# Reordering bias reads and three conversion steps at the start of an attention stage

## The chip, the cores and the metric

The kernel runs on one core of one Trainium2 chip. The metric is the device time of one execution in microseconds. Three runs of the kernel before gave 890.56, 889.25 and 890.60 us, with a median of 890.56 us. The engines are TensorE (PE, its weight load is PEld), VectorE (DVE), ScalarE (ACT), GpSimd (POOL) and SyncE (SP), whose queue issues nearly all DMA transfers here.

## What the kernel computes

Three stages follow one another. The first is attention with a learned relative-position bias over 4 batches, 8 heads, 576 positions and 64 dimensions a head:

```
scores = scale * q @ k.T                                # [4, 8, 576, 576]
x      = log1p(|i - j|) / log1p(max(i, 1))              # [576, 576]
bias   = relu(x * w1 + b1) @ w2                         # [576, 576, 8]
attn   = softmax(scores + bias) @ v
```

Then come a gated block, `((x @ w1) * (x @ w2)) @ w3 @ w_out` on 2304 rows, and a second block of an input projection, a softmax-weighted unit, a normalisation and an output projection. Weights arrive as 64-bit words and are turned into 32-bit numbers on the chip in five steps each.

## The kernel before, in words

The bias is made first, in 36 steps (`Bias.run`, L168). One step makes 16 rows of the bias for all heads: VectorE and ScalarE make masks (L162, L160), TensorE sums them (L191), ScalarE or VectorE copies the sum to a tile `rs` (L198, L196), and SP writes that tile to one of three DRAM tensors, `bias_d` (`write`, L47 through `Chip.load`). The steps take the rows in the order `list(range(32, 36)) + list(range(32))`, so that rows 384 to 511, the row groups 24 to 31, are written by the last eight steps, 28 to 35. After each step `beside(n)` puts other work in the queues: the first query, key and value tiles, bias reads, and steps of the first weights' conversion (`EARLY`).

Attention then runs over 16 pairs (four head pairs by four batches) of ten rounds each. Round s belongs to pair n = s // 10, and k = s % 10 is its unit. Units 0 to 8 are one 128 by 576 tile of scores each; round 9 has none. In a round (`slot`) the program hands each engine, in this order, the work of tiles of different ages: ScalarE copies transposed tiles (L478) and takes the exponential of the tile of two rounds ago (L381); VectorE adds the bias to the tile of the round before (L374), makes inverse sums (L388, L389), and makes the low parts of the transposed tiles (L492); GpSimd scales tiles (L393); TensorE makes the scores (L363, or L79 to L81 for unit 0), the transposes of a tile of eight rounds ago (L403) and the products with the values (L446). Each engine works through its own queue in order.

SP issues in order too. Query and key tiles are split by GpSimd into a high and a low part (L54, L57) and copied by SP into the layout that TensorE needs (`prep`; L51): the query copies (four `q<-qh`, two `qz<-ql`) of pair n + 1 go out in the third round of pair n, its four key copies `k<-kr` in the fifth, behind the load of the query and key tile of the pair after (`qkr`, 640 KB). What goes out in a round is kept in a list, `later[s]`, which `slot(s)` empties in order. Pair 1's first score tile with copied keys is that of round 11.

`load_bias(p, k)` has SP read the bias rows of unit k from `bias_d`. Units 1 to 4 are the first head's rows, 5 to 8 the second's; unit 4 and unit 8 take rows 384 to 511, unit 3 and unit 7 rows 256 to 383. A read of unit 4 is one DMA of 288 KB, one of unit 7 or 8 two DMAs of 256 and 32 KB. A read has to wait until the writes of its rows have landed.

The five conversion steps of the first two weight tiles (`first_ab`) are ten instructions in a list, which `some(n)` hands out: two behind bias step 29, five behind step 33, and the last three behind round 4 (`FILL`): one of line 72 and two of line 73, each a VectorE operation on 128 by 512 words with two inputs in SBUF. Their results are read after the last score round, from round 161 on.

Of the kernel before, what the change touches and what calls it, by code (L numbers as in the profile page):

```python
# [202 lines left out]
class Attention:  # L203
# [6 lines left out]
    LAG = 8  # L210
    AVLAG = 2
    EARLY = {29: 2, 33: 5}
    FILL = 4
    AHEAD = {(2, 3): (1,), (2, 7): (3,), (3, 3): (0,), (3, 5): (5,), (3, 8): (7,)}

    def __init__(self, ch, i, bias, x_d, ga):
# [255 lines left out]
    def slot(self, s):  # L472
        NP = len(self.pairs)
        n, k = divmod(s, 10)
        SQ = self.SQ
        ev, self.EV = self.EV, []
        for hi, lo, src in ev:
            self.nc.scalar.copy(hi, src)  # L478
        while self.OUT:
            self.nc.scalar.copy(*self.OUT.pop())  # L480
        if s - 2 in SQ:
            self.exp(*SQ[s - 2])
        if s - 1 in SQ:
            self.add_bias(*SQ[s - 1])
        if s - 3 in SQ:
            self.inverse(*SQ[s - 3])
            if SQ[s - 3][1] % 2:
                self.normalise(*SQ[s - 4])
            if SQ[s - 3][1] % 2 or SQ[s - 3][1] == 8:
                self.normalise(*SQ[s - 3])  # L490
        for hi, lo, src in ev:
            self.nc.vector.tensor_tensor(out=lo, in0=src, in1=hi.bitcast(F), op=ALU.subtract)  # L492
        if n < NP and k < 9:
            self.scores(n, k)
        tn, tu = divmod(s - self.LAG, 10)
        if 0 <= tn < NP:
            for u in self.TU[tu]:
                self.transposes(tn, u)
        an, au = divmod(s - self.LAG - 1 - self.AVLAG, 10)
        if 0 <= an < NP:  # L500
            self.values(an, self.AV[au], s)
        if k == 4 and n + 2 < NP:
            self.load_qk(n + 2)
        for fn in self.later.pop(s, []):
            fn()
        if n < NP:
            if n + 1 < NP and k < 4:
                self.prep(n + 1, k, s + 1)
            if k in (5, 6):
                self.prep(n, k - 1, s + 1)  # L510
            if k == 7 and n + 1 < NP:
                self.load_v(n + 1)
            p, b = self.pairs[n]
            if p + 1 < NPH:
                for j in self.AHEAD.get((b, k), ()):
                    self.load_bias(p + 1, *((j, j + 1) if j else (0,)))
            if s == self.FILL:
                self.some(len(self.fill))


class Gated:
# [735 lines left out]
def tile_kernel(tc, i, out):  # L1257
    with tc.manual_schedule(), tc.tile_pool(name="dram", bufs=1, space=DRAM) as dp:
        x_d = [dp.tile([2, DM, S], F, name="x_d%d" % b) for b in range(NB)]
        x2_d = [dp.tile([DM, TC], F, name="x2_d%d" % c) for c in range(NC)]  # L1260
        gw_d = dp.tile([FF, DM], F, name="gw_d")
        g_d = [dp.tile([FF, TC], F, name="g_d%d" % c) for c in range(NC)]
        ch = Chip(tc)

        ga = Gated(ch, i, x_d, x2_d, gw_d, g_d)
        ga.open_keep()
        bias = Bias(ch, i, dp)
        bias.open()
        at = Attention(ch, i, bias, x_d, ga)
        at.open_left()  # L1270

        at.load_qk(0)
        for n in range(2):
            at.load_ab(n)
        at.load_v(0)

        def beside(n):

            at.start(n)
            if n == 7:  # L1280
                at.load_bias(0, 0)
            if n in (24, 27):
                at.load_bias(0, *{24: (1, 2), 27: (5, 6)}[n])
            if n in (32, 33):
                at.load_bias(0, {32: 3, 33: 7}[n])
            at.some(at.EARLY.get(n, 0))

        bias.run(beside)
        bias.ctx.close()
        at.open_right()  # L1290
        scored = 10 * len(at.pairs)
        for s in range(at.slots()):
            n = s - scored
            if n == 0:
                at.left.close()
                at.psl.close()
                ga.open_left()
            if n == ga.MID:
                at.top.close()
                ga.open_mid()  # L1300
            if s == 3:
                at.load_bias(0, 4)
                at.load_bias(0, 8)
            at.slot(s)
            ga.early(n)
        at.right.close()
        at.psr.close()
        ga.open_right()
        ga.run()
        ga.tail.close()  # L1310
        ga.psr.close()
        ga.psl.close()
        so = Solu(ch, i, ga, out)
        so.open()
        so.run()
        so.ctx.close()
        ga.right.close()
        ga.left.close()
# [64 lines left out]
```

## Time and profile before

| | |
|---|---|
| profiled execution | 891.37 us |
| its span | 889.6 us |
| median of three runs | 890.56 us |
| TensorE, VectorE, ScalarE, GpSimd busy | 96%, 72%, 57%, 35% of the span |
| mean granted TensorE clock | 0.994 of full speed |

The span runs from the first instruction to the last; 1.77 us of the profiled execution lie around it. A time such as 64.86 is counted from the start of the span. Bias steps fill the first 59 us, attention goes on to about 310 us. In a row of a timeline the start comes first, then how long it took; "[5.64 <-DVE st L374]" says that the engine had idled 5.64 us and what ended that. For a DMA, the row of SP is its issue; "us to landing" is from the start of the issue to the end of the transfer.

### The profile page before, as it was taken

To read this page: it belongs to the slowest core of one execution; us is meant where nothing else is said; L and a number is where in the kernel's file an instruction comes from. 1 tells how busy PE (TensorE), PEld (TensorE's weight loads), DVE (VectorE), ACT (ScalarE), POOL (GpSimd) and SP (SyncE) were. 2 spreads that over 40 slices of the span, in tenths; PEclk is the share of its full clock that TensorE was granted. 3 is DMA by queue.
4 is the path that set the end of the run, shared out by engine and by line. 5 is a ranking of instruction groups with operands and counts; after the bars stand their busy time and mean duration, and the time that the engine had idled before them with its cause. 6 is when DMAs were issued, how large, how long until landed. Compare 5 with 4: busy or idle time off the path is not lost.

```text
span 889.6 us, 15987 instructions
## 1 busy us (share of the span) xinstructions
PE 853.7 (96%) x5430; PEld 769.2 (86%) x5430; DVE 638.0 (72%) x1517; ACT 506.0 (57%) x1073; POOL 307.9 (35%) x379
## 2 busy tenths in 40 slices
PE   7978999999999889989999999999999999999998
PEld 3548999999999789888888999999998788888886
DVE  8998999999999788997652777353454855555552
ACT  6887999999899845443322445333344544444432
POOL 3038888889898700000000000000344333333300
PEclk9998999999999999999999999999999999999999
DMA  6997897897987656767413587443134011111001
GB/s 227 300 304 184 240 268 200 252 261 192 302 222 211 189 169 210 229 216 230 157 60 133 189 278 257 152 166 122 63 131 128 27 42 41 44 40 48 24 24 48
DMA packets 93538, 146.31 MB, mean 164 GB/s; under 512 B 11792, under 2 KB 58256, under 8 KB 93456
## 3 DMA queue, kind: packets, MB, share of 16 engines
q1 hardware_dynamic: 86064, 134.96, 49.7%
q10 hardware_dynamic: 7392, 10.33, 3.3%
q8 instruction: 43, 0.70, 0.3%
q14 instruction: 39, 0.32, 0.1%
HBM read 81.93 MB, written 41.30 MB: 139 GB/s over the span
## 4 chain that ended last, share of the span: by engine, by line
PE 78%; DVE 8%; ACT 2%; DMA 2%; issue 2%; SPq 0%; POOL 0%; ACTq 0%; DVEq 0%; POOLq 0%
PE op L446 9%; PE tp L403 8%; PE sp L363 7%; PE ab L79 7%; PE ab L81 7%; PE ab L80 7%; PE o L80 4%; PE o L79 4%; PE o L81 4%; PE x L80 3%; PE x L81 3%; PE x L79 3%; PE hx L79 2%; PE hx L80 2%; PE hx L81 2%
## 5 line engine op out<-in xcount | busy, mean ns | idle before, releaser
L79 PE MATMUL ab<-x,ab 128*128 128x384 f32 x320 | 109.0, 341 | 5.1 <-DVE a L791 5.1
L492 DVE TENSOR_TENSOR etl<-tp,eth 128x512 fp32r<-128x512 f32 (+1 forms) x160 | 99.4, 630 | 14.0 <-ACT eth L478 11.8
L81 PE MATMUL ab<-x,ab 128*128 128x384 f32 x320 | 108.0, 337 | 1.1 <-DVE ab L650 1.1
L80 PE MATMUL ab<-x,ab 128*128 128x384 f32 x320 | 107.9, 337 | 0.1
L393 POOL TENSOR_SCALAR e<-e,st 128x576 f32<-128x576 f32 x128 | 95.0, 752 | 27.6 <-DVE st L389 24.7
L381 ACT ACTIVATE e<-e,st 128x576 f32<-128x576 f32 x128 | 100.1, 782 | 6.1 <-DVE st L374 6.1
L478 ACT CAST eth<-tp 128x512 fp32r<-128x512 f32 (+1 forms) x160 | 85.2, 543 | 22.6 <-PE tp L403 16.1
L374 DVE CUSTOM_DVE_ANT_0 e<-sp,bt 128x576 f32<-128x576 f32 x128 | 95.5, 747 | 3.2 <-DMA bt<-bias_d 1.9
L403 PE MATMUL tp<-idt,e 128*128 128x128 f32 x576 | 87.3, 274 | 4.3 <-DVE ell L492 1.6
L940 POOL MEMSET onef<- 128x128 f32 x1 | 0.2, 204 | 232.0 <-DVE mean L925 232.0
L363 PE MATMUL sp<-k,q 128*128 128x288 f32 x256 | 73.5, 302 | 7.3 <-DVE st L374 6.1
L403 PEld LDWEIGHTS tp<-idt,e 128*128 128x128 f32 x576 | 69.5, 141 | 6.7 <-DVE ell L492 1.8
L363 PE MATMUL sp<-k,qz 128*128 128x288 f32 x256 | 72.4, 298 | 0.0
L791 DVE TENSOR_TENSOR a<-ab,a 128x384 f32<-128x384 f32 x48 | 26.6, 555 | 63.6 <-ACT a L790 63.3
L79 PEld LDWEIGHTS ab<-x,ab 128*128 128x128 f32 x320 | 60.4, 189 | 8.2 <-DVE a L791 8.2
L446 PE MATMUL op<-eth,v 128*128 128x288 f32 x256 | 65.6, 337 | 0.4 <-ACT o L480 0.4
L80 PE MATMUL x<-gl,wf 128*128 128x384 f32 x192 | 64.7, 337 | 0.5 <-DVE gl L62 0.5
L81 PE MATMUL x<-gh,wf 128*128 128x384 f32 x192 | 64.5, 336 | 0.0
L79 PE MATMUL x<-gh,wf 128*128 128x384 f32 x192 | 64.5, 336 | 0.0
L81 PEld LDWEIGHTS ab<-x,ab 128*128 128x128 f32 x320 | 60.3, 189 | 1.6 <-DVE ab L650 1.4
L80 PEld LDWEIGHTS ab<-x,ab 128*128 128x128 f32 x320 | 60.4, 189 | 0.4 <-DVE x L750 0.4
L1231 ACT ACTIVATE o<-o,st 128x512 f32<-128x512 f32 x18 | 12.4, 688 | 79.5 <-PE o L81 29.4
(213 smaller groups left out, 2341.4 us busy)
## 6 DMA issues: line engine op xcount, KB each, us to landing
bias_d<-rs SPq DMA_DIRECT2D x36, 295.5 KB, 4.1
qkr<-in_qk SPq DMA_DIRECT2D x16, 640.0 KB, 5.6
k<-kr SPq DMA_DIRECT2D x64, 144.0 KB, 5.6
g_d<-a ACTq DMA_DIRECT2D x48, 192.0 KB, 2.8
gl<-g_d SPq DMA_DIRECT2D x48, 192.0 KB, 2.6
x_d<-o SPq DMA_DIRECT2D x58, 144.0 KB, 4.0
q<-qh SPq DMA_DIRECT2D x64, 128.0 KB, 2.7
raw<-in_wo SPq DMA_DIRECT2D x16, 512.0 KB, 4.3
```

The lines of the kernel that those rows point to most:

```text
L79: mm(out, a[0], b[0], start=first, stop=False, skip_group_check=more)
L80: mm(out, a[0], b[1], start=False, stop=False, skip_group_check=more)
L81: mm(out, a[1], b[0], start=False, stop=last, skip_group_check=more)
L363: nc.tensor.matmul(ps[:, half, :HS], w[("q", "qz")[x]][:, h, q * 128 : q * 128 + 128], w["k"][:, h, half * HS : half * HS + HS], start=x = ...
L374: self.nc.vector.tensor_tensor_reduce(out=halves(e), in0=ps[:, :, :HS], in1=halves(self.BT[(self.pairs[n][0], k)]), scale=-0.125, scalar=3e38,
L381: self.nc.scalar.activation(e, e, AF.Exp, bias=st[:, c : c + 1], scale=-1.0, accum_out=st[:, 2 + 2 * c : 3 + 2 * c])
L393: self.nc.gpsimd.tensor_scalar(out=e, in0=e, scalar1=st[:, c : c + 1], scalar2=1.0, op0=ALU.mult, op1=ALU.mult)
L403: tr = lambda c, src: nc.tensor.transpose(ps[: src.shape[1], c * 128 : c * 128 + 128], src, self.idt)
L446: nc.tensor.matmul(w["op"][:, half, :HS], lhs, rhs, start=c == 0 and x == 0, stop=c == 4 and x == 1)
L478: self.nc.scalar.copy(hi, src)
L492: self.nc.vector.tensor_tensor(out=lo, in0=src, in1=hi.bitcast(F), op=ALU.subtract)
L791: nc.vector.tensor_tensor(out=a, in0=ps[:, 1, :TC], in1=a, op=ALU.mult)
```

## The change

The read of unit 4's bias rows for the first head pair is no longer issued behind all six query copies of round 2, but as the third of that round's list, behind two of them. The two DMAs of unit 7 leave bias step 33 and stand ahead of round 3, where unit 4's read was, before those of unit 8. The last three conversion steps leave round 4 for rounds 20, 30 and 40, one each.

```diff
-    FILL = 4
+    FILL = (20, 30, 40)
...
-            if s == self.FILL:
-                self.some(len(self.fill))
+            if s in self.FILL:
+                self.some(1)
...
-            if n in (32, 33):
-                at.load_bias(0, {32: 3, 33: 7}[n])
+            if n == 32:
+                at.load_bias(0, 3)
             at.some(at.EARLY.get(n, 0))
...
+            if s == 2:
+                at.later[s].insert(2, lambda: at.load_bias(0, 4))
             if s == 3:
-                at.load_bias(0, 4)
+                at.load_bias(0, 7)
                 at.load_bias(0, 8)
             at.slot(s)
```

## Rows read from the trace of the kernel before

**Rows 1.** Busy time by stretch: us, five engines, granted clock, DMA share, GB/s.

```profile
68.00:70.00 2.00, 0.80 (x3) 0.80 (x4) 1.59 (x6) 0.82 (x3) 0.00 (x0) 0.50 0.97 183
...
76.00:300.00 224.00, 222.94 (x1763) 218.85 (x1763) 208.28 (x608) 206.76 (x490) 196.80 (x223) 1.00 0.81 226
...
310.00:312.00 2.00, 1.18 (x8) 0.95 (x8) 2.00 (x4) 1.42 (x4) 1.22 (x2) 1.00 0.35 118
312.00:314.00 2.00, 1.51 (x7) 1.51 (x8) 2.00 (x5) 0.67 (x2) 0.00 (x0) 0.59 0.03 9
```

**Rows 2.** Chain of waits around the idle stretch: start, us, what.

```profile
64.86 3.38 DMA bt<-bias_d
...
69.20 3.51 PE sp L363 x12
...
75.96 0.77 PE sp L363 x4
```

**Rows 3.** Timelines of TensorE and VectorE, 69 to 106 us.

```profile
69.20 0.61 PE L363 MATMUL sp<-k,q 128*128 128x288 f32 x1 [5.64 <-DVE st L374]
...
71.52 0.76 DVE L374 CUSTOM_DVE_ANT_0 e<-sp,bt 128x576 f32<-128x576 f32 x1 [0.20 <-PE sp L363]
...
75.41 0.45 DVE L492 TENSOR_TENSOR ell<-sp,elh 64x64 fp32r<-64x64 f32 x2
...
106.01 0.29 PE L363 MATMUL sp<-k,q 128*128 128x288 f32 x1
```

**Rows 4.** SP's issues and the last `rs` on ScalarE, 58 to 68 us.

```profile
58.15 0.93 SPq L47 DMA_DIRECT2D bt<-bias_d  x2
...
58.44 0.76 ACT L198 ACTIVATE rs<-ps,cst 128x591 f32<-128x591 f32 x1
...
59.68 0.45 SPq L47 DMA_DIRECT2D bias_d<-rs  x1
...
62.95 1.23 SPq L51 DMA_DIRECT2D q<-qh  x2
...
67.44 0.59 SPq L51 DMA_DIRECT2D k<-kr  x1
```

**Rows 5.** KB, us to landing; issued 56.43, 57.78, 58.62, 59.68, 64.86, 67.44.

```profile
bias_d<-rs SPq DMA_DIRECT2D x1, 295.5 KB, 3.1
...
bias_d<-rs SPq DMA_DIRECT2D x1, 295.5 KB, 3.7
...
bt<-bias_d SPq DMA_DIRECT2D x1, 32.0 KB, 3.9
...
bias_d<-rs SPq DMA_DIRECT2D x1, 295.5 KB, 4.5
...
bt<-bias_d SPq DMA_DIRECT2D x1, 288.0 KB, 3.4
...
k<-kr SPq DMA_DIRECT2D x1, 144.0 KB, 7.8
```

**Rows 6.** The same, issued 77.82, and second key copies issued 99.06 and 129.81.

```profile
q<-qh SPq DMA_DIRECT2D x1, 128.0 KB, 2.2
...
k<-kr SPq DMA_DIRECT2D x1, 144.0 KB, 6.4
...
k<-kr SPq DMA_DIRECT2D x1, 144.0 KB, 5.0
```

**Rows 7.** VectorE's conversion steps and a GpSimd scaling beside them, timelines.

```profile
62.88 1.90 DVE L72 SCALAR_TENSOR_TENSOR rab<-rab 128x512 uint32<-128x512 uint32 x1
64.71 1.75 DVE L73 SCALAR_TENSOR_TENSOR rab<-rab 128x512 uint32<-128x512 uint32 x2
...
64.23 1.69 POOL L393 TENSOR_SCALAR eab<-eab,st 128x576 f32<-128x576 f32 x1
```

**Rows 8.** Such a scaling, 80 to 160 us (busy, mean ns, idle); line 72 elsewhere (ns).

```profile
L393 POOL TENSOR_SCALAR eab<-eab,st 128x576 f32<-128x576 f32 x6 | 4.5, 748 | 0.0
...
L72 DVE SCALAR_TENSOR_TENSOR cm<-raw,cm x46: 674/692/694, 313.6 to 556.5; 128x512 uint32<-128x512 uint32 x46
```

## The prediction

> **What bounds the kernel now.** I read the busy time by stretch first. From 76 to 300 us TensorE works 222.94 of 224 us [rows 1]: behind round 11 attention has no room, and what is lost or won before it arrives at the end nearly whole. So the question is when round 11 starts. The chain of waits shows the last gap ahead of it: the DMA of unit 4's bias rows, issued at 64.86, lands 3.38 us later [rows 2], and TensorE idles 5.64 us until 69.20 [rows 3]. During it the granted clock fell to 0.50 [rows 1], the lower of its levels (1.2 against 2.4 GHz), and twelve score products from 69.20 took 3.51 us [rows 2], where four take 0.77 from 75.96 on.
>
> Round 11's scores start at 75.96 [rows 2]. They need three things. VectorE must have emptied a score buffer: its two operations from 75.41 end at 75.86 [rows 3], and that came last. Second, the query copies. Third, the first two key copies: the second was issued at 67.44 [rows 4] and landed 7.8 us later [rows 5], at 75.2. The two ends that matter stand only 0.6 us apart. That decides this case: cutting the bias wait gains 0.6 us at most as long as the key copies land when they do.
>
> **Unit 7's two DMAs leave step 33.** Their issue takes SP 0.93 us at 58.15 [rows 4], just ahead of the last two bias writes. The last `rs` is ready at 58.44 + 0.76 = 59.20 [rows 4], so the last write goes out at about 59.23 where it went out at 59.68 [rows 4]. On the DMA engines, which are full there, the write issued at 57.78 landed at 61.5, unit 7's last read at 58.62 + 3.9 = 62.5, and the last write at 59.68 + 4.5 = 64.2 [rows 4, 5]. Without the 1.0 us of the reads that last write lands at about 63.2. Bounds: 59.23 + 3.1 = 62.3 by the quickest such write [rows 5], and 64.2 if nothing changes. I take 63.2, for the engines were full.
>
> **Unit 4's read moves past four query copies.** Two copies and their pitch are 1.23 us [rows 4], so four are 2.5 us, and the place itself comes at about 62.0. But unit 4's rows are those of the last eight bias steps, so the read has to wait for that last write, at the head of SP's queue, and whatever stands behind it there waits too. So it is issued at 63.2, not at 62: 1.65 us earlier than 64.86. It then takes between 2.2 us, which a query copy takes in a quiet stretch [rows 6], and its own 3.4 us [rows 5]. I take 3.1, nearer to its own row, since the last write's successors are still moving. It lands at 66.3 (65.4 to 67.6) instead of 68.24, and rounds 5 to 10 come 1.9 us sooner: round 11 could start at about 74.0.
>
> The Trainium skill (DMA: Bandwidth & Descriptors, "Anatomy of one DMA", measured for DMAs that GpSimd issues) counts a fixed 2.0 us plus the bytes at 436 GB/s. By it, as an estimate, 288 KB would take 2.7 us and land at 65.9; by the row it is 66.6. Neither end would move the start of round 11, by what follows.
>
> **What is late next: the key copies.** They stand in the same queue behind all of this. From unit 4's issue to that of the second key copy it was 67.44 - 64.86 = 2.58 us [rows 2, 4]. Now there are four query copies (2.5 us) and unit 7's two DMAs (1.0 us with the pitch) between them besides: 63.2 + 2.5 + 1.0 + 2.6 = 69.3 us, 1.85 us later than 67.44. Of its 7.8 us [rows 5] some was the backlog of full DMA engines (share 0.97 at 68 to 70 [rows 1]); the same copy of later pairs takes 6.4 or 5.0 [rows 6]. The wait of about 1.2 us in SP lets that backlog shrink, while the bytes ahead of the keys stay the same. I take 7.0: between the copy's own row and the 6.4. So it lands at 76.3; bounds 69.3 + 5.0 = 74.3 and 69.3 + 7.8 = 77.1. Round 11 starts at 76.35: **0.4 us later than before** (bounds -1.6 and +1.2), though the bias came 1.9 us sooner.
>
> **Unit 7's read, now late.** It goes out at 63.2 + 0.6 + 2.5 = 66.3 and with 3.4 lands at 69.7. VectorE took unit 7 at 71.52 [rows 3], 3.3 us behind the bias's landing; now that is 66.3 + 3.3 = 69.6. A wait of 0.1, bounds 0 and 1, lies inside the 2.3 us by which the keys are later than the rest, and costs nothing. If the keys were early, it would cost its length.
>
> **The three conversion steps.** In round 4 they ran from 62.88 to 66.46 [rows 7], under the wait for the bias, for nothing; under a bias that lands at 66.3 they would cost 0.1 to 0.2 us, which the keys hide too. Taking them away gains nothing. In rounds 20, 30 and 40 there is no wait to hide them, but in these rounds VectorE has no tile of a unit 9 to add bias to, and in 224 us it idles 15.7 [rows 1], about 1 us in each pair of 15.0 us (round 11 at 75.96, round 31 at 106.01 [rows 2, 3]). One step takes 0.69 undisturbed [rows 8] and up to 1.90 beside GpSimd [rows 7]. So each costs between 0 and about 0.9; I take 0.1, as 0.69 is under 1, and 0.3 for the three. A gain is excluded there: work is only added.
>
> **The sum.** 0.4 + 0.3 = +0.7 us. The profiled execution would go from 889.6 + 1.77 = 891.37 to 892.1. It lies 0.81 above the median of 890.56, so the median becomes **891.3 us**. A measurement of this kernel can tell about 0.2%, 1.8 us: no change that can be told.
>
> **The rivals.**
>
> A second drop of the clock (the other side). TensorE now idles twice, about 3.7 us for the bias and 2.3 us for the keys. The 5.64 us cost it the clock, and so did a stretch where it worked 1.18 of 2 us, after which the clock was 0.59 [rows 1]. If the wait for keys makes it fall, rounds 11 to 13 run at half. Twelve products at half took 3.51 us [rows 2], at full they are some 1.6 to 2.3 (0.77 for four, with the start of the first): a price of 1.2 to 1.9, 1.5 here. That gives 890.56 + 0.7 + 1.5 = 892.8, slower. It decides from a keys' wait of some 2 us on. Against it: 2.3 us is under half of 5.64.
>
> Conversion steps that meet GpSimd. Line 72 took 1.90 for 0.69, and the scaling beside it 1.69 for 0.75 [rows 7, 8]. If each of the three delays the products with the values by 0.9, the sum is 0.4 + 2.7: 893.7. Against it is VectorE's idle time. The Trainium skill (GPSIMD Engine Reference, "1. Specifications") says that GpSimd shares its SBUF interfaces with VectorE and contends with VectorE instructions of two SBUF inputs, as these three are. The trace agrees by the 1.69 us; by that rule the steps leave an empty stretch for one where GpSimd works 197 of 224 us [rows 1], and this rival is the time.
>
> Keys land early. If DMAs drain while SP waits, the second key copy lands in 5.0 us, at 74.3, and round 11 starts there: -1.6 + 0.3, 889.3. For it: later pairs. Against: every byte ahead of the keys is still there.
>
> The change doesn't do what it says. If the last write still lands at 64.2, unit 4's read goes out 0.6 us sooner only, and the keys 2.85 later, landing at up to 78.1: +1.5 to +2.1 with keys as slow as 7.0 to 7.8 us and no loss elsewhere, 892.3. Against it are the 1.0 us of DMA time that left.
>
> **How the numbers follow.** Forecast 0.42, with its own range 890.2 to 892.2; clock 0.25; GpSimd 0.08; keys early 0.17; no earlier read 0.08. Faster than 888.8 would take keys as early as the bound and no cost of the steps, or a gain that I don't see: 0.13. Slower than 892.3: most of the clock's case, GpSimd's, half of the last: 0.33. Between: 0.54. The range from 888.7 to 893.1 leaves about 0.1 out on each side.
>
> **What would show it.** Right: SP issues unit 4's read right behind two query copies, close to the landing of the last bias write at about 63.2; TensorE's first gap is about 3.7 us instead of 5.64; a new gap stands ahead of round 11's scores, ended by the key copies' landing near 76.3; VectorE has three lone operations of lines 72 and 73 near 91, 106 and 121 us, with no gap of TensorE behind them. Wrong: round 11's scores before 75, or a read of unit 4 that is issued before the last write has landed; then the gain is up to 1.9 us and more, and the time below 889.

## The result, and the profile after

The changed kernel is slower: a median of 894.22 us over 7 runs against 890.23 us over 7 runs of the kernel before, a ratio of 1.0054 (95% interval 1.0040 to 1.0069). Its profiled execution took 894.85 us, with a span of 893.1 us.

SP's issues in the changed kernel, start and us:

```profile
59.88 1.36 SPq L51 DMA_DIRECT2D q<-qh  x2
63.20 0.33 SPq L47 DMA_DIRECT2D bt<-bias_d  x1
...
66.04 2.05 SPq L47 DMA_DIRECT2D bt<-bias_d  x4
68.19 0.38 SPq L47 DMA_DIRECT2D qkr<-in_qk  x1
...
69.12 0.59 SPq L51 DMA_DIRECT2D k<-kr  x1
```

Its transfers issued at 58.81 (the last bias write), 63.20 (unit 4's read) and 69.12 (the second key copy), with KB and us to landing:

```profile
bias_d<-rs SPq DMA_DIRECT2D x1, 295.5 KB, 4.2
...
bt<-bias_d SPq DMA_DIRECT2D x1, 288.0 KB, 3.5
...
k<-kr SPq DMA_DIRECT2D x1, 144.0 KB, 8.6
```

Both query copies are out at 61.24. Then SP stands still for 1.96 us until the last bias write has landed, at 58.8 + 4.2 = 63.0, and issues unit 4's read at 63.20. That read lands at 66.7, against 68.24 before [rows 2]. The second key copy goes out 1.7 us later than before [rows 4] and lands at 69.12 + 8.6 = 77.7, against 75.2 before [rows 5].

The busy time by stretch, with the columns of [rows 1]:

```profile
62.00:64.00 2.00, 1.16 (x8) 0.79 (x6) 0.54 (x4) 1.28 (x4) 1.92 (x3) 1.00 0.28 76
...
68.00:70.00 2.00, 2.00 (x9) 1.75 (x8) 1.31 (x6) 1.44 (x5) 1.25 (x2) 0.50 0.93 252
...
72.00:74.00 2.00, 0.44 (x2) 0.14 (x1) 0.75 (x3) 1.97 (x7) 1.17 (x2) 1.00 1.01 230
74.00:76.00 2.00, 1.93 (x10) 1.87 (x10) 1.92 (x10) 0.90 (x3) 0.89 (x2) 0.64 0.98 198
76.00:78.00 2.00, 0.36 (x2) 0.00 (x0) 1.65 (x6) 0.58 (x1) 1.97 (x3) 0.50 0.58 151
78.00:80.00 2.00, 1.97 (x9) 1.98 (x10) 0.63 (x1) 0.00 (x0) 2.00 (x3) 0.50 0.69 169
...
312.00:314.00 2.00, 1.82 (x15) 1.59 (x15) 1.60 (x3) 2.00 (x5) 2.00 (x2) 1.00 1.05 347
```

While SP stands still the DMA engines run nearly dry: a share of 0.28 and 76 GB/s from 62 to 64 us, where the kernel before had 1.04 and 361:

```profile
62.00:64.00 2.00, 1.49 (x8) 1.13 (x8) 1.97 (x7) 1.66 (x5) 1.92 (x2) 1.00 1.04 361
```

The granted clock, back at 1.00 from 72 to 74 us, falls a second time, to 0.64 and 0.50 from 74 to 80 us.

TensorE and VectorE between the gap and the later rounds (idle time before an instruction in brackets):

```profile
67.69 0.61 PE L363 MATMUL sp<-k,q 128*128 128x288 f32 x1 [4.53 <-DVE st L374]
...
74.07 0.40 PE L79 MATMUL sp<-kr,qh 128*128 128x288 f32 x1 [1.24 <-DVE st L374]
74.31 0.30 PE L80 MATMUL sp<-kr,qh 128*128 128x288 f32 x1
...
74.82 0.44 PE L80 MATMUL sp<-kr,qh 128*128 128x288 f32 x1
...
78.03 0.58 PE L363 MATMUL sp<-k,q 128*128 128x288 f32 x1 [1.68 <-DMA vr<-in_v]
...
94.42 0.29 PE L363 MATMUL sp<-k,q 128*128 128x288 f32 x1
...
187.42 0.37 PE L363 MATMUL sp<-k,q 128*128 128x288 f32 x1 [1.30 <-DMA k<-kr]
...
292.93 0.29 PE L363 MATMUL sp<-k,q 128*128 128x288 f32 x1
...
73.25 0.76 DVE L374 CUSTOM_DVE_ANT_0 e<-sp,bt 128x576 f32<-128x576 f32 x1 [2.20 <-DMA bt<-bias_d]
```

The first gap shrank from 5.64 to 4.53 us. Two new ones follow: VectorE waits 2.20 us for unit 8's rows, of which TensorE feels 1.24, and round 11's scores wait 1.68 us. The clock falls between these two: the same product takes 0.30 us at 74.31 and 0.44 at 74.82, while the wait for the keys begins at 76.35 only. The profile puts that last wait down to a load of values, but this load, issued at 71.76, took 7.5 us and landed at 79.3. The landing that fits is that of the second key copy at 77.7: in this run and in e2, e3, e4, e5 and e13 below, round 11 starts 0.3 to 0.4 us behind it, whatever the profile names.

Round 11 starts at 78.03 against 75.96 [rows 2], 2.07 us later. Round 21 starts at 94.42 against 91.05, 3.37 us later: the 1.3 us between are rounds 11 and 12, which run at half clock until about 81.4.

Round 151 starts at 292.93 against 287.45, 5.5 us later, after three waits for key copies in later pairs (2.1 us in all, the longest the 1.30 at 187.42), where the kernel before shows one wait of 0.8 us. In the runs below that leave the later pairs as they are, such waits sum to between nothing (e5) and 2.8 us (e13), so these 2.1 us are not shown to come from the change. At the end of attention 2 us come back: there the kernel before lost half its clock at 312 [rows 1], and this one did not. That is not shown to be the change's doing either: the profile of e7 has that fall (0.50 from 312 to 314 us), those of e2, e3 and e5 have not. The span grew by 3.5 us.

### The profile page after: what moved, and what is told of

Read it like the earlier page. It is cut to its first block, busy times and chain, and to the rows that moved or that the text cites. A ratio compares the mean times of both kernels' runs of the same rounds, so it can differ in the third digit from the quotient of the medians.

```text
span 893.1 us, 15989 instructions
## 1 busy us (share of the span) xinstructions
PE 854.9 (96%) x5430; PEld 769.8 (86%) x5430; DVE 638.1 (71%) x1517; ACT 506.8 (57%) x1073; POOL 308.1 (35%) x379
## 4 chain that ended last, share of the span: by engine, by line
PE 70%; DVE 11%; DMA 6%; ACT 3%; issue 2%; POOL 1%; SPq 0%; ACTq 0%; DVEq 0%; POOLq 0%
PE op L446 7%; PE ab L79 7%; PE ab L81 6%; PE ab L80 6%; PE sp L363 6%; PE tp L403 6%; PE o L80 4%; PE o L79 4%; PE o L81 4%; PE x L80 3%; PE x L81 3%; PE x L79 3%; DMA k<-kr 2%; PE t L1215 2%; PE hx L80 2%
## 5 line engine op out<-in xcount | busy, mean ns | idle before, releaser
L791 DVE TENSOR_TENSOR a<-ab,a 128x384 f32<-128x384 f32 x48 | 26.7, 555 | 63.5 <-ACT a L790 63.2
L363 PEld LDWEIGHTS sp<-k,q 128*128 128x128 f32 x256 | 49.3, 193 | 11.4 <-DVE st L374 6.0
```

The costliest lines, as they stand in the source:

```text
L363: nc.tensor.matmul(ps[:, half, :HS], w[("q", "qz")[x]][:, h, q * 128 : q * 128 + 128], w["k"][:, h, half * HS : half * HS + HS], start=x = ...
L791: nc.vector.tensor_tensor(out=a, in0=ps[:, 1, :TC], in1=a, op=ALU.mult)
```

## The experiments

Each was timed in 5 rounds against the kernel before on the same chip; ratios are to it, with 95% intervals.

**e1: the conversion steps alone.**

```diff
-    FILL = 4
+    FILL = (20, 30, 40)
...
-            if s == self.FILL:
-                self.some(len(self.fill))
+            if s in self.FILL:
+                self.some(1)
```

> The three conversion steps go to rounds 20, 30 and 40; all bias reads stay as before. Theory A (unit 4's read waits for the last bias write at the head of SP's queue, the DMA engines run dry, the key copies of pair 1 land late): no change, ratio 1.000 to 1.001, round 11's scores at about 76. Theory C (the conversion steps in busy rounds cost the time): ratio 1.002 to 1.004 and gaps of TensorE behind rounds 20, 30 and 40.

Ratio 1.0010 (0.9998 to 1.0022). Line 73's two steps, with their shortest, median and longest duration in ns:

```profile
L73 DVE SCALAR_TENSOR_TENSOR rab<-rab x2: 1080/1082/1083, 106.4 to 121.9; 128x512 uint32<-128x512 uint32 x2
```

They take 1.08 us beside GpSimd, and 0.69 where it rests. TensorE waits for VectorE behind them nowhere for more than 0.2 us. So theory C is out as the main cause: by the ratio 0.10 of the 0.54% is the steps', by its interval between nothing and 0.22.

**e2: both bias reads, conversion steps as before.** The change's diff without `FILL`.

> Both bias reads move as in the change; the conversion steps stay behind round 4. Theory A: the whole loss stays, ratio 1.003 to 1.006, the second key copy lands at 77 or later, a gap of 1.5 us or more ahead of round 11's scores. Theory C: at most half of the loss, ratio 1.000 to 1.002.

Ratio 1.0040 (1.0027 to 1.0053). Its round 11:

```profile
76.81 0.37 PE L363 MATMUL sp<-k,q 128*128 128x288 f32 x1 [2.70 <-DMA vr<-in_v]
```

The second key copy, issued at 68.44, took 8.0 us and landed at 76.4, sooner than the 77 that A gave, but the gap is beyond its 1.5 us. The reads carry most of the loss, as theory A had it.

**e3: unit 4's read alone.**

```diff
+            if s == 2:
+                at.later[s].insert(2, lambda: at.load_bias(0, 4))
             if s == 3:
-                at.load_bias(0, 4)
                 at.load_bias(0, 8)
```

> Only unit 4's read moves behind two query copies; unit 7's reads stay behind bias step 33, the conversion steps behind round 4. Theory A: SP stands still until the last write has landed at about 64.2, the keys are issued near 69.2 and land at 76.5 to 77.5: ratio 1.001 to 1.004. Theory B (what costs is that unit 7's two reads now stand ahead of the keys): the keys are no later than before, ratio 0.998 to 1.000.

Ratio 1.0015 (0.9999 to 1.0031): inside what A gave, but not clear of no change. In SP's queue of this run the standing still is seen alone, from 62.35 to 64.38:

```profile
60.67 1.68 SPq L51 DMA_DIRECT2D q<-qh  x2
64.38 0.33 SPq L47 DMA_DIRECT2D bt<-bias_d  x1
...
64.00:66.00 2.00, 0.00 (x0) 0.00 (x0) 2.00 (x3) 0.00 (x0) 2.00 (x3) 1.00 0.43 75
...
77.55 0.46 PE L363 MATMUL sp<-k,q 128*128 128x288 f32 x1 [2.00 <-DVE st L389]
...
k<-kr SPq DMA_DIRECT2D x1, 144.0 KB, 7.7
```

The second key copy, issued at 69.50, took 7.7 us and landed at 77.2. Theory B, by which the keys would be no later here, fails on this, as far as one profile goes: the profiled run, 894.03 us, is the slowest of its twelve, whose median is 891.00.

**e4: unit 7's reads alone.**

```diff
-            if n in (32, 33):
-                at.load_bias(0, {32: 3, 33: 7}[n])
+            if n == 32:
+                at.load_bias(0, 3)
...
             if s == 3:
                 at.load_bias(0, 4)
+                at.load_bias(0, 7)
                 at.load_bias(0, 8)
```

> Only unit 7's reads move, from bias step 33 to behind unit 4's read, which stays behind all six query copies; the conversion steps stay behind round 4. Theory A: SP never stands still for a write, the DMA engines stay full from 60 to 70 us and the bytes ahead of the keys are the same: second key copy at 75 to 76, ratio 0.999 to 1.001. Theory B: second key copy at 76.5 or later, ratio 1.002 to 1.005.

Ratio 1.0001 (0.9985 to 1.0018), as A had it. The second key copy landed at 74.8, a little ahead of the 75 to 76 that A gave:

```profile
64.00:66.00 2.00, 0.00 (x0) 0.00 (x0) 1.63 (x2) 0.00 (x0) 2.00 (x2) 0.79 0.88 216
...
75.19 0.37 PE L363 MATMUL sp<-k,q 128*128 128x288 f32 x1 [0.87 <-DMA vr<-in_v]
...
k<-kr SPq DMA_DIRECT2D x1, 144.0 KB, 7.7
```

**e5: the changed kernel with rows that had landed.** Unit 4 of the first head pair reads rows 256 to 383.

```diff
-            self.bias.read(t, row, 2 * p, 0)
+            self.bias.read(t, 256 if (p, k) == (0, 4) else row, 2 * p, 0)
```

> The changed kernel, but unit 4 of the first head pair is read from rows 256 to 383, which landed long before, so that SP has nothing to wait for (the bias of that unit is then another one; amount and shape of the transfer are the same). Theory A (SP standing still empties the DMA engines and brings the keys late): unit 4's read is issued near 61.5, DMA share in 62 to 64 us goes from 0.28 to over 0.7, second key copy issued near 68 and landed at 75 to 76, ratio 1.000 to 1.002. Theory B (the two reads more ahead of the keys and their order are enough): second key copy at 77 or later, ratio 1.003 to 1.006.

Ratio 1.0029 (1.0013 to 1.0045), above what A gave and at the edge of B. SP no longer stands still, and the DMA share from 62 to 64 us is 0.88:

```profile
61.83 0.58 SPq L47 DMA_DIRECT2D bt<-bias_d  x1
62.51 0.46 SPq L51 DMA_DIRECT2D qz<-ql  x1
...
76.30 0.37 PE L363 MATMUL sp<-k,q 128*128 128x288 f32 x1 [2.62 <-DMA vr<-in_v]
...
k<-kr SPq DMA_DIRECT2D x1, 144.0 KB, 7.6
```

The second key copy, issued at 68.31, lands at 75.9, as A had it, and the profiled round 11 is 0.3 us late only. But the profiled run, 890.51 us, is the fastest of its twelve, whose median is 893.40: it doesn't show what the others lost. TensorE idles 2.62 us ahead of round 11 in it, and yet its clock stays at 1.00 from 72 to 82 us. Over the 12 timed runs the mean granted clock was 0.9935, against 0.9948 for the kernel before in the same rounds. At half clock a share of 0.0026 more of 890 us is 2.3 us, which costs 1.2 us or 0.13%. With the 0.1% of the conversion steps that comes near the 0.29%; but a mean over a run doesn't say where in it the clock fell, so that the gap ahead of round 11 made it fall in the slower runs is not shown. What e5 does show is that standing still is not the whole cause.

**e13: unit 4's read alone, of rows that had landed.** e3 and e5's edit together.

> Unit 4's read behind two query copies as in the change, but from rows 256 to 383 that landed before (that unit's bias is another one); unit 7's reads stay behind step 33 and the conversion steps behind round 4. SP neither stands still nor issues more ahead of the keys. Theory A (a cost only where the keys come later): keys issued and landed as before (67.4, 75.3), round 11's scores at 75.4 to 76, ratio 0.999 to 1.001. Theory D (the second gap itself costs, because TensorE's clock drops in it or behind it even when the keys are no later): ratio 1.001 to 1.003.

Ratio 0.9991 (0.9980 to 1.0002), as A had it, though by its own profile the keys were not "as before": the second key copy, issued at 68.34, took 8.0 us and landed at 76.3, and round 11 came later than the 75.4 to 76 expected:

```profile
76.69 0.37 PE L363 MATMUL sp<-k,q 128*128 128x288 f32 x1 [1.32 <-DMA k<-kr]
```

The gap ahead of round 11 is 1.32 us here and the mean clock 0.9953. An early read that neither stands still nor sits with two more reads ahead of the keys costs nothing, and it does not gain anything clear of no change either: the keys still end the wait. So a loss clear of the noise comes only where both reads have moved, in the change, e2 and e5; of either alone (e3, e4, e13) none is shown.

**e7: the changed kernel, key copies ahead of the 640 KB load for pair 1.**

```diff
-        if k == 4 and n + 2 < NP:
+        if k == 4 and 0 < n < NP - 2:
             self.load_qk(n + 2)
         for fn in self.later.pop(s, []):
             fn()
+        if s == 4:
+            self.load_qk(2)
```

> The changed kernel with pair 1's four key copies ahead of pair 2's 640 KB load in SP's queue, all else the same. Theory A says that the keys' landing is the whole path: second key copy lands at 72 to 73.5, round 11's scores start at 75.5 to 76.5, behind unit 8's bias; ratio 0.999 to 1.002 (the conversion steps stay). If another thing than the keys made the changed kernel slow, the ratio stays at 1.004 to 1.006.

Ratio 1.0003 (0.9988 to 1.0018). SP still stands still in this run, and unit 4's read still goes out at 62.56; but the second key copy, issued at 68.42, takes 4.0 us instead of 8.6, and no gap stands ahead of round 11:

```profile
67.86 2.40 SPq L51 DMA_DIRECT2D k<-kr  x4
70.30 0.59 SPq L47 DMA_DIRECT2D qkr<-in_qk  x1
...
73.81 0.37 PE L363 MATMUL sp<-k,q 128*128 128x288 f32 x1
...
k<-kr SPq DMA_DIRECT2D x1, 144.0 KB, 4.0
```

With one transfer moved and all else of the change left in, the loss is gone: what costs is that the keys stand behind the 640 KB load. Round 11 starts at 73.81, sooner than the 75.5 to 76.5 expected. Two things limit the reading. VectorE began unit 8's tile at 71.48 here, against 73.25 in the changed kernel, so the load's place brought unit 8's rows sooner as well, and e7 doesn't part the two. And a move that gains by itself would have shown the same; e10 below answers that: made in every pair of the kernel before, it gained 0.18% (0.06 to 0.31), where e7 took back some 0.5%.

**e8: filling SP's wait.** From the kernel before: unit 7's reads third in round 2's list, unit 4's behind four copies, e7's edit.

```diff
+            if s == 2:
+                at.later[s].insert(4, lambda: at.load_bias(0, 4))
+                at.later[s].insert(2, lambda: at.load_bias(0, 7))
             if s == 3:
-                at.load_bias(0, 4)
                 at.load_bias(0, 8)
```

> From the kernel before: unit 7's reads go behind two query copies (they fill SP's wait), unit 4's read behind four, pair 1's key copies ahead of pair 2's load; conversion steps behind round 4. Theory A: unit 4's read is issued at 62.5 to 63.3 without SP standing still, lands near 66; keys land before 73.5; round 11's scores at 73.5 to 74.5, ratio 0.997 to 0.999. If the head of line and the keys are not what costs, ratio 1.000 or above.

Ratio 1.0003 (0.9990 to 1.0016): a miss. Unit 4's read went out at 63.46 without a stop, but behind unit 7's 288 KB it took 4.9 us and landed at 68.3, no sooner than before, so that the run says nothing against the keys. VectorE's first instruction with it:

```profile
68.45 0.76 DVE L374 CUSTOM_DVE_ANT_0 e<-sp,bt 128x576 f32<-128x576 f32 x1 [2.46 <-DMA bt<-bias_d]
```

**e9 to e12: key copies ahead of the load in every pair.**

```diff
-        if k == 4 and n + 2 < NP:
-            self.load_qk(n + 2)
         for fn in self.later.pop(s, []):
             fn()
+        if k == 4 and n + 2 < NP:
+            self.load_qk(n + 2)
```

e9 puts it on e8 in place of e7's edit, e10 on the kernel before, e11 on e2 (both reads of the change), e12 on e4 (unit 7's reads alone).

> As the one before, but in every pair the key copies go ahead of the load of the pair after next. The short gaps ahead of the second unit's scores of later pairs (0.3 to 1.3 us each, ended by k<-kr) should go too: ratio 0.995 to 0.998. If those gaps come from something else, the ratio is that of the one before.

> The kernel before with the key copies of every pair ahead of the load of the pair after next. In the kernel before the keys are not what round 11 waits for (VectorE at 75.86 is), so round 11 stays at about 75.9; only the gaps ahead of the second unit of later pairs can go. Theory A: ratio 0.998 to 1.000.

> Both bias reads as in the change, conversion steps behind round 4, key copies ahead of the load in every pair. Theory A: the bias comes 1.5 us sooner and the keys no longer stand in the way, round 11's scores near 74: ratio 0.997 to 0.999. If the drained DMA engines cost in another way, 1.000 or above.

> Only unit 7's reads move (behind unit 4's, which stays behind all six query copies), conversion steps behind round 4, key copies ahead of the load in every pair. SP never stands still for a write; the bias comes about 0.9 us sooner against the first score; round 11's scores near 74.5: ratio 0.996 to 0.999, the best of these if SP's standing still costs anything besides the keys.

The ratios are 0.9991 (0.9978 to 1.0004), 0.9982 (0.9969 to 0.9994), **0.9960 (0.9948 to 0.9973)** and 0.9968 (0.9955 to 0.9981). All but e9 are faster than the kernel before, and e11 and e12 beat both kernels; e9 fell short of its expectation as e8 did, and e11 did better than its own. e10 and e11 differ by the change's own two bias reads. Behind the load those reads cost 0.40% (e2 against the kernel before); with the keys out of the way they cost nothing: 888.23 us in e10, 886.92 in e11, 0.15% less, though that gain is not clear of the noise of 12 and 5 runs. e11's waits of TensorE for more than a moment from 80 to 296 us, then its first gap, round 11 and the second key copy:

```profile
PE tp L403 <- POOL e L393: 0.6, 2, 0.4
...
66.18 0.61 PE L363 MATMUL sp<-k,q 128*128 128x288 f32 x1 [4.05 <-DVE st L374]
...
73.36 0.37 PE L363 MATMUL sp<-k,q 128*128 128x288 f32 x1
...
k<-kr SPq DMA_DIRECT2D x1, 144.0 KB, 4.5
```

No wait for a key copy is left in any pair. The difference between e11 and e12 is inside their intervals, so whether SP's standing still costs anything besides late keys stays open.

## Why the prediction was wrong

The forecast was 891.3 us, a change too small to tell, in a range up to 893.1; it came out at 894.22 us. The path was the forecast's own: the keys, in SP's queue behind the moved reads, set the start of round 11. Two of its terms were mis-sized, and the rival that came with them was held too unlikely.

- *Round 11 decides, and the keys stand in the same queue.* Right: round 11 starts 0.3 to 0.4 us behind the second key copy in six runs, and e7 takes the loss away by moving the load behind the keys.
- *Unit 7's reads leave, the last write lands at 63.2; unit 4's read goes out then and lands at 66.3.* Right: 63.0, 63.20 and 66.7. The first gap was 4.53 us and not about 3.7: TensorE reached it 0.4 us sooner than in the kernel before, and the bias landed 0.4 us later than forecast.
- *The second key copy goes out at 69.3.* Right: 69.12.
- *"I take 7.0" for its landing.* This is the step that failed. It took 8.6 us, outside the bound of 7.8, so the keys landed at 77.7 instead of 76.3 and round 11 started 2.07 us later than before, not 0.4. Of the 1.7 us between, 1.6 are the landing, and 0.3 are the step from it to round 11, which the forecast put at 0.05; the issue at 69.12 gave 0.2 back. The reason that I gave, that SP's wait lets a backlog shrink, was the wrong one. In e3, e4, e5 and e13, with the DMA engines nearly dry (a share of 0.43 from 64 to 66 us in e3) or full beforehand (0.88 in e4), the copy behind the 640 KB load took 7.6 to 8.0 us; ahead of that load it took 4.0 to 5.0 in e7, e8, e11 and e12. So the load in front of it makes some 3 us of its time, and SP's wait none that shows. The lower values of later pairs should not have been mixed in: their copies stand behind such a load too, and why they land sooner, and why this one took 8.6 us and not 7.6 to 8.0, stays open.
- *Unit 7's read late by 0 to 1 us.* Unit 7 was not late, but unit 8, behind it, was: VectorE waited 2.20 us for it. I had not looked at unit 8. The keys came later still, so that it did not move round 11; but the clock fell right behind it.
- *The clock's second drop*, a rival at 0.25, came true in the profiled run: 0.64 and 0.50 from 74 to 80 us, and 1.3 us more between rounds 11 and 21, where 1.5 was priced. It did not come as I had it, by a keys' wait of "some 2 us": it fell ahead of that wait, right behind the one for unit 8's rows, of which the forecast had nothing. In e2 and e3 the profiled clock fell behind the keys' gap (0.50 from 78 to 80 us, gaps of 2.70 and 2.00); in e5, with 2.62, and e13, with 1.32, it stayed at 1.00. Over the runs the mean clock was 0.9923 in the changed kernel, 0.9934 in e2, 0.9935 in e5 and 0.9945 in e3, against 0.9953 in e4 and e13. What a gap here costs of the clock differs from run to run, and when it does stays open.
- *The conversion steps* cost 0.3 in the forecast; e1 shows 0.1%, 0.9 us, with an interval from -0.2 to 2.0. Each took 1.08 to 1.11 us instead of 0.69. The rule of the Trainium skill (GPSIMD Engine Reference, "1. Specifications") that a VectorE instruction with two SBUF inputs contends with GpSimd agrees with that stretching; but the rival built on it, 0.9 us for each, did not come.

The near-match of the two profiles, 3.5 us of span against 4.0 us of the medians, is in part luck: the 2.1 us lost in later pairs and the 2 us that came back at the end of attention, neither of them tied to the change, cancel. In the forecast's own terms, 2.07 us of keys and 1.3 of the clock, by this profile, and 0.9 of the steps, by e1, make 4.3 us, where 0.7 was forecast.

By size: in e2, round 11 stands 18.50 us behind the first score with copied keys of pair 0 (58.31 to 76.81), in the kernel before 16.56 (59.40 to 75.96). That is 1.9 us or 0.22%. The mean clock of 0.9934 against 0.9950 gives another 1.4 us or 0.16%. Together 0.38%, and 0.40% was measured. That sum rests on one profile each and on a mean clock, which doesn't say where in the kernel the clock fell, so it is an account, not a proof.

## What to carry to other kernels

When a transfer is moved forward in an in-order DMA queue, look first at what it has to wait for, and then at who stands behind it: its wait becomes theirs. Before shortening a wait, find the second thing that ends at nearly the same time; here the two lay 0.6 us apart. Moving that one (small copies ahead of a large load that nobody needs yet) took the loss away in e7 and, in every pair of the kernel before, gained 0.2% in e10. A wait that is cut in two can cost more than its length: in the changed kernel's profile the clock fell twice around rounds 4 to 13, where the kernel before lost it once there, though in the profiles of e5 and e13, with two waits as well, it fell once only.

## What the runs showed of the hardware

Pair 1's second key copy, of 144 KB, took 4.0 to 5.0 us ahead of a 640 KB load and 7.6 to 8.6 us behind it, whether the DMA engines had been full or nearly idle before. In later pairs the key copies took 5.5 us in the median behind such a load (the changed kernel, 80 to 300 us) and 2.8 us ahead of it (e10).

The moved rate of full DMA engines was not one figure: at shares of 0.93 to 1.01 they moved 198 to 252 GB/s in three stretches between 68 and 76 us in the changed kernel, and 361 GB/s in the kernel before from 62 to 64. I did not find out why.
